# FNet mixing and a gated feed-forward on one core: where four units' halves of sums and two pairs' feed-forward operands stand

## The chip, the cores and the metric

The kernel runs on one core of a Trainium2 chip. Five engines work side by side, each through its own queue and in the order of its program: TensorE (PE) multiplies matrices, VectorE (DVE), ScalarE (ACT) and GpSimd (POOL) work on elements, SyncE (SP) starts the transfers. They wait for each other by semaphores; an instruction that waits holds up all that stands behind it in its queue. The metric is the device time of one execution in microseconds (us), lower is better.

## The reference

With S = 2048 rows, D = 448 columns and 1792 hidden columns:

```python
a = jnp.einsum("bsd,ed->bse", x, dft_hid_re)      # x is layernorm(A_x)
b = jnp.einsum("bsd,ed->bse", x, dft_hid_im)
y = jnp.einsum("ts,bse->bte", dft_seq_re, a) - jnp.einsum("ts,bse->bte", dft_seq_im, b)
...
h = A_x + y
g = jnp.einsum("bsd,df->bsf", x, w_gate)           # here x is layernorm(h)
u = jnp.einsum("bsd,df->bsf", x, w_up)
h2 = h + jnp.einsum("bsf,fd->bsd", gelu(g) * u, w_down)
```

The inputs are 32-bit floats, drawn at random; the four DFT matrices (cosines and sines) are inputs too.

## The kernel before

**Numbers.** Each 32-bit operand is split into two 16-bit halves: a high half, which ACT rounds (`hi_part`, L108), and a low half, the rest, which DVE subtracts (`lo_part`, L112 without and L114 with a scale). A product takes three matmuls: high by high, high by low, low by high.

**Stages.** First comes the sequence DFT: W (the cosine and sine matrices, `dft_seq`) times the normed rows xs. It runs in 64 steps, `for n in range(N_STEPS)`. Each step multiplies one *unit* of W, a 128 x 1024 piece that SP loads (`seq_load`, tile `wr`) and ACT and DVE split (tile `ws`). Then, pair by pair of row blocks (a pair p has the halves g = 0 and 1), comes the hidden DFT (`hid_mm(p, g)`, PE, L730, 21 matmuls). It follows in the same 64 steps as soon as a pair is through. Then the gate and up products and the down products run in two more loops, from about 346 us on.

**Units.** Up to step 27 a step is 24 plain matmuls (L644, tile `acc`). From `FAST` = 28 on a step is 42 matmuls of half the width (L521, tile `acc_f`) in Strassen's form: a unit has raw halves (`fast_raw`, tile `ws28_0` for unit 28, from `wr`) and four sums of its blocks (`fast_sums`, DVE, L471 to L473), whose halves `fast_split` makes (two ACT instructions and one of DVE, tile `ws28_1`). The other factor is xs, raw, and its sums T: for row pair j POOL adds (`t_sums(j)`, L575 to L581, tiles `tx`), ACT and DVE split (`t_hi(j)`, `t_lo(j)`, tile `t`). Step 28 reads T of j = 0 and 1, step 29 of 2 (first half) and 3 (second half), and so on. Units 28, 29 and 30 are made in steps 24, 26 and 27 (`fast_at`); from unit 31 on, unit n + 2 is made in step n. Of a unit's tile `wr` there are five buffers, which the sums share; of `ws` there are six.

**The hidden product's seed.** `hid_mm(p, g)` adds to a bank `y` that ACT fills before (`hid_seed(p, g)`, L711, scaled h). There is one such bank. So `hid_seed(p, 1)` waits until ACT has drained `hid_mm(p, 0)` (`hid_out`, L719 to L721), and `hid_mm(p, 1)` waits for the seed. For pair 1, `hid_mm(1, 0)` stands behind the first half of step 24, `hid_mm(1, 1)` behind the first half of step 25.

**Feed-forward operands.** For each of the first four pairs the normed h is made into operands of the gate and up products inside these steps: `ffn_norm_act` (ACT, L243), `ffn_sums` (six of DVE, L254 to L263, tile `tt`), `ffn_split` (four of ACT, six of DVE, tile `xs_`), `ffn_transpose` (four transposes of SP, L305). The steps stand in a table, `n0, n1, n2` for the normed h, the sums and the split; the transposes follow in steps n2 + 1 and n2 + 2.

**Order.** It is written by hand. In each step `n` all engines get, in this order: loads and halves of plain units; for `n in fast_at` the unit's sums and halves; what `early[n]` lists; the first half of the matmuls; `after[n, 0]`; the second half; `after[n, 1]`. Other work in these lists that the prediction speaks of: the gate weights (`Weights.sums`, `gu_s`, L328 to L331; `split`, `gu_w`), the drain of a finished plain pair (`z_out`, tile `zs`), SP's transposes of it (`z_turn`, L669), and the drain of a finished fast pair at the end of each fourth fast step (`fast_out`, tile `e`, L550 and L553). `t_hi(5)` stands in `after[24, 1]`, `t_hi(3)` in `after[27, 1]`, `t_lo(3)` in `after[28, 0]`.

Of the kernel before, what the change touches and what calls it, by code (L numbers as in the profile page):

```python
# [32 lines left out]
def kernel(  # L33
# [73 lines left out]
    def hi_part(dst, src, scale=1.0):  # L107
        A.activation(dst, src, AF.Copy, scale=scale)  # L108

    def lo_part(dst, src, hi, scale=1.0):  # L110
        if isinstance(scale, float) and scale == 1.0:
            V.tensor_sub(dst, src, hi)  # L112
        else:
            V.scalar_tensor_tensor(dst, src, scale, hi, op0=ALU.mult, op1=ALU.subtract)  # L114
# [304 lines left out]
    def step_of(n):  # L419

        k, qq = divmod(n - NT, 4)
        return 2 + k // 2, k % 2, qq

    def seq_load(n):
        wr[n] = dft.tile([P, 8 * P], F32, tag="wr", bufs=5, name=f"wr{n}")
        if n < NT:
            nc.sync.dma_start(wr[n].rearrange("p (b t) -> p b t", b=4), w_seq[8 * (n % 2) + n // 2])
            return
        p, part, qq = step_of(n)
        for i in range(2):  # L430
            dst = wr[n][:, i * 4 * P : (i + 1) * 4 * P].rearrange("p (g t) -> p g t", g=2)
            nc.sync.dma_start(dst, w_seq[8 * p + 2 * qq + i][:, 2 * part : 2 * part + 2, :])
# [19 lines left out]
    FAST = N_STEPS - 36  # L452
# [6 lines left out]
    def fast_views(n):  # L459
        raw = wr[n].rearrange("p (i b t) -> p i b t", i=2, b=4)  # L460
        s = fast_s[n].rearrange("p (s i t) -> p s i t", s=4, i=2)
        src = raw[:, :, 0:3].rearrange("p i b t -> p i (b t)")
        dst = fast_w[n][0][:, :, : 6 * P].rearrange("p l (i b) -> p l i b", i=2)
        return raw, s, src, dst
# [17 lines left out]
    def fast_raw(n):  # L482

        raw, s, src, dst = fast_views(n)
        hi_part(dst[:, 0], src, D_SC)
        lo_part(dst[:, 1], src, dst[:, 0], D_SC)

    def fast_split(n):

        w = fast_w[n][1]  # L490
        for part in slice(0, 4 * P), slice(4 * P, 8 * P):
            hi_part(w[:, 0, part], fast_s[n][:, part], D_SC)
        lo_part(w[:, 1], fast_s[n], w[:, 0], D_SC)
# [208 lines left out]
    def h_tile(q, j):  # L702
        hp[q, j] = pair_tile(f"hx{q}_{j}", 2 * (q - 2) + j if q > 1 else j)
        nc.sync.dma_start(hp[q, j], xr[q // 2, 2 * (q % 2) + j])
# [3 lines left out]
    def hid_seed(p, g):  # L708

        y = ys[p, g] = ps_tr.tile([P, 512], F32, tag="tr", name=f"y_{p}_{g}")  # L710
        A.activation(y[:, :D], hp[p // 2, p % 2][:, g, :], AF.Copy, scale=sign_of(p, g) * D_SC)  # L711
# [31 lines left out]
    def h_store(q, j):  # L743
        nc.sync.dma_start(h_dram[2 * q + j], hp[q, j])
# [10 lines left out]
    early, after = {}, {}  # L755

    def at(where, n, *what):
        where.setdefault(n, []).extend(what)
# [25 lines left out]
    for p, (n, half) in enumerate(turns):  # L784
        b, j = divmod(p, 2)
        m = (19, 24, 29, 36, 44, 52, 60)[p]
        last = ((20, 0), (25, 0), (31, 0), (38, 0), (48, 0), (56, 0), (61, 1))[p]
        m1 = last[0] + 1
        at(early, m - 4, lambda b=b, j=j: h_tile(b, j))
        at(early, m - 2, lambda p=p: hid_seed(p, 0))  # L790
        for g in range(2):

            place = last if g else (m, 0)
            at(after, place, lambda p=p, g=g: hid_mm(p, g), lambda p=p, g=g: hid_out(p, g))
            if g == 0:
                at(after, (m, 0), lambda p=p: hid_seed(p, 1))
        at(after, (n, half), lambda p=p: z_turn(p))
        at(early, m1 + p // 3 if p < 5 else N_STEPS - 7 + p, lambda b=b, j=j: ffn_rstd(b, j))
        at(after, (m1, 0), lambda b=b, j=j: h_store(b, j))
        if b < 2:  # L800

            n0, n1, n2 = ((21, 22, 23), (27, 28, 32), (36, 37, 38), (44, 45, 46))[p]
            at(early, n0, lambda b=b, j=j: ffn_bias(b, j), lambda b=b, j=j: ffn_norm_act(b, j, hp[b, j]))
            at(early, n1, lambda b=b, j=j: ffn_sums(b, j))
            at(early, n2, lambda b=b, j=j: ffn_split(b, j))
            for k in range(4):
                at(after, (n2 + 1 + k // 2, k % 2), lambda b=b, j=j, k=k: ffn_transpose(b, j, (k,)))
# [47 lines left out]
    for n in range(N_STEPS):  # L855
        if n == 0:
            for key in first:
                seq_acc(*key, last=key == first[-1])
        elif n >= FAST and n % 4 == 0:
            fast_begin(n)  # L860
        elif n >= NT and n % 4 == 0:
            for g in range(2):
                seq_acc(*step_of(n)[:2], g)
        if n + 3 < NT:
            x_load(n + 3)
        for unit in range(n + 5 + (n > FAST - 6), min(n + 6 + (n > FAST - 7), FAST + 2)):
            seq_load(unit)

        if 0 < n < FAST - 3:
            seq_hi(n + 3)  # L870
        if 0 < n < NT - 2:
            x_rstd(n + 2)
            x_hi(n + 2)
            x_norm(n + 2)
        if 0 < n < NT - 3:
            x_stats(n + 3)
        if n == 0:
            seq_lo(2)
        if n + 3 < FAST:
            seq_lo(n + 3)  # L880
        if n in fast_at:
            unit = fast_at.index(n) + FAST
            fast_sums(unit)
            while last_lo:
                last_lo.pop()()

            if n < FAST or n % 4 < 3:
                fast_raw(unit)
                fast_split(unit)
                if unit + 2 < N_STEPS:  # L890
                    seq_load(unit + 2)
        if n == 0:
            x_stats(3)
            x_lo(2)
        if 0 < n < NT - 2:
            x_lo(n + 2)
        for what in early.get(n, ()):
            what()
        if n >= FAST:

            last = n % 4 == 3
            one = [(i, k) for k in range(7) for i in range(2)] if last else [(i, k) for i in range(2) for k in range(7)]
            if n % 4 == 0 and n > FAST:

                one = [(i, k) for i in range(2) for k in range(5)] + [(i, k) for i in range(2) for k in (5, 6)]
            for m, (i, k) in enumerate(one):
                fast_mm(n, i, k)
                if last and i == 1 and k in (0, 2, 4, 6):  # L910
                    fast_out(n, k)
                    if n < N_STEPS - 1:
                        unit = n + 2
                        if k == 2:
                            fast_raw(unit)
                        elif k == 4:
                            fast_split(unit)
                            if unit + 2 < N_STEPS:
                                seq_load(unit + 2)
                if m in (6, 13):  # L920
                    for what in after.get((n, m // 7), ()):
                        what()
            continue

        if n < NT:
            one = [(key, n - n % 2 + key[0], 2 * (2 * key[1] + key[2]) + n % 2, n) for key in first]
            if n == 0:

                order = [(0, m) for m in (0, 2, 1)] + [(1, m) for m in range(3)]
                one = [(*a, (m,)) for jj, m in order for a in one[4 * jj : 4 * jj + 4]]  # L930
            elif n < 6:
                one = [(*a, (m,)) for m in (0, 2, 1) for a in one]
            else:
                one = [(*a, range(3)) for a in one]
        else:
            p, part, qq = step_of(n)
            one = [
                ((p, part, g), n, 4 * i + 2 * g + c, 4 * qq + 2 * i + c, range(3))
                for i in range(2)
                for g in range(2)  # L940
                for c in range(2)
            ]
            if qq == 3:

                one.sort(key=lambda a: a[0])
        for half in range(2):
            for key, unit, block, c, terms in one[half * len(one) // 2 : (half + 1) * len(one) // 2]:
                seq_mm(key, ws[unit], block, c, terms)
                if c == NT - 1 and 2 in terms and (n < NT or block in (5, 7)):
                    z_out(*key)  # L950
            for what in after.get((n, half), ()):
                what()
# [376 lines left out]
    for t in range(NF):  # L1329
        w = gu.get(t + 2) if t + 2 in JIT_F else None  # L1330
        n = PREP_AT.get(t)
# [88 lines left out]
    for t in range(NF, N_GU):  # L1420
# [37 lines left out]
        if ends:  # L1458
            p = now[-1] // NC
# [21 lines left out]
        for p, t0 in ended.items():  # L1481
            each = 3 if p < 3 else 2
            n = each * (t - t0)
# [106 lines left out]
```

## Time and profile before

| | us |
|---|---|
| time, median of 3 runs (709.05 to 711.11) | 709.29 |
| the profiled execution's own time | 708.99 |
| its span, first to last instruction | 707.2 |
| PE busy | 692.3 |
| DVE, ACT, POOL busy | 586.1, 397.4, 171.8 |

A row in order of time gives the start (us from the span's start), the length of the group of like instructions, engine, line, operation, what is written and read, its shape and the count; in brackets stand the idle time of the engine ahead of it and what ended it. The row of a group reaches to the end of its last instruction, and the next one of PE begins some 0.2 us before that, so stretches of PE are taken from start to start. Steps can be found by counting matmuls: 24 of L644 for a step up to 27, 42 of L521 from step 28, 21 of L730 for a hidden product.

### The profile page before, as it was taken

The page shows a single profiled execution, that of the slowest core. Times are in us where ns is not written, and L with a number is a line of the kernel's source. Part 1 is how long each engine was busy: PE and PEld are TensorE (multiplying, and loading weights), DVE is VectorE, ACT ScalarE, POOL GpSimd, SP SyncE. Part 2 cuts the span into 40 slices and gives each one's busy share as a digit, 9 for nine tenths or more (in the row PEclk, how much of TensorE's full clock was granted, in tenths as well). Part 3 has the DMA queues.
Part 4 walks back from the last instruction along what each step waited for, and adds up shares of the span by engine and source line. Part 5 has one row for each costly group of instructions (what it writes and reads, how often), then busy time and mean ns, then how long its engine had stood idle before and what let it go on. Part 6 is the DMA issues. An engine that isn't in the chain of part 4 may idle for free.

```text
span 707.2 us, 14130 instructions
## 1 busy us (share of the span) xinstructions
PE 692.3 (98%) x5380; PEld 521.2 (74%) x5380; DVE 586.1 (83%) x1156; ACT 397.4 (56%) x789; POOL 171.8 (24%) x183
## 2 busy tenths in 40 slices
PE   9999999599999999999999999999999999999998
PEld 6555555248888889888744444469999999999997
DVE  7998996969799899998576798877677876899886
ACT  5776655455566475654646666655546454555531
POOL 0005745732010100000213333511120111232224
PEclk9999999989999999999999999999999999999999
DMA  8788689883785829484775879797788985887612
GB/s 273 250 231 285 136 286 252 223 193 104 182 201 140 212 78 223 161 187 155 222 254 183 280 255 253 204 323 232 233 250 297 262 280 182 302 295 262 237 54 79
DMA packets 113444, 153.99 MB, mean 218 GB/s; under 512 B 61664, under 2 KB 78176, under 8 KB 113376
## 3 DMA queue, kind: packets, MB, share of 16 engines
q1 hardware_dynamic: 113376, 153.09, 72.5%
q8 instruction: 42, 0.69, 0.4%
q14 instruction: 26, 0.21, 0.1%
HBM read 104.82 MB, written 34.34 MB: 197 GB/s over the span
## 4 chain that ended last, share of the span: by engine, by line
PE 89%; DVE 6%; issue 2%; ACT 2%; DMA 1%; POOL 0%; SPq 0%; DVEq 0%; ACTq 0%; POOLq 0%
PE acc L644 17%; PE acc_d L1252 15%; PE acc_f L521 15%; PE pY L1048 15%; PE pX L1048 9%; PE pZ L1048 9%; PE y L730 8%; DVE ws L114 2%; DVE sums L471 1%; ACT ws L108 1%; PE pw L102 1%; DVE e L550 1%; DVE sums L472 1%; DMA wr<-in_w_seq_dram 1%; DVE xs L112 0%
## 5 line engine op out<-in xcount | busy, mean ns | idle before, releaser
L1048 PEld LDWEIGHTS <-gw 128*128 128x128 f16 x1287 | 125.8, 98 | 33.6
L521 PEld LDWEIGHTS <-ws 128*128 128x128 f16 x1512 | 144.7, 98 | 3.8 <-DVE ws L114 1.8
L644 PE MATMUL acc<-xs,ws 128*128 128x448 f16 x672 | 127.9, 352 | 0.0
L1142 POOL TENSOR_TENSOR hs<-hs,c 128x256 f32<-128x256 f32 (+1 forms) x42 | 61.3, 1460 | 244.7 <-ACT c L1140 192.5
L644 PEld LDWEIGHTS <-ws 128*128 128x128 f16 x672 | 65.7, 98 | 61.2
L1252 PE MATMUL acc_d<-wd,dn_w 128*128 128x224 f16 x1008 | 110.6, 259 | 0.0
L521 PE MATMUL acc_f<-t,ws 128*128 128x224 f16 x864 | 103.8, 259 | 0.4 <-DVE ws L114 0.4
L1252 PEld LDWEIGHTS <-dn_w 128*128 128x128 f16 x1008 | 96.9, 98 | 1.9
L114 DVE SCALAR_TENSOR_TENSOR ws<-wr,ws 128x768 f16<-128x768 f32 (+2 forms) x66 | 73.4, 1114 | 15.3 <-ACT ws L108 14.9
L521 PE MATMUL acc_f<-xs,ws 128*128 128x224 f16 x648 | 82.8, 259 | 0.7 <-DVE ws L114 0.7
L1048 PE MATMUL pY<-hops,gw 128*128 128x256 f16 (+1 forms) x561 | 81.9, 289 | 0.0
L730 PE MATMUL y<-wh,z 128*128 128x448 f16 x336 | 67.5, 357 | 9.2 <-ACT y L711 9.2
L1048 PEld LDWEIGHTS <-gu_w 128*128 128x128 f16 x351 | 34.2, 98 | 40.9
L108 ACT ACTIVATE ws<-wr 128x768 f16<-128x768 f32 (+2 forms) x66 | 59.4, 902 | 8.2 <-DMA wr<-in_w_seq_dram 6.9
L108 ACT ACTIVATE ws<-sums 128x512 f16<-128x512 f32 x72 | 43.4, 623 | 33.8 <-DVE sums L471 28.2
L730 PEld LDWEIGHTS <-z 128*128 128x128 f16 x336 | 33.2, 99 | 39.3 <-issue 11.0
L1048 PE MATMUL pX<-hops,gw 128*128 128x256 f16 (+1 forms) x363 | 56.3, 289 | 0.0
L1048 PE MATMUL pZ<-hops,gw 128*128 128x256 f16 (+1 forms) x363 | 56.3, 289 | 0.0
L1093 ACT ACTIVATE pY<-pX 128x256 f32<-128x256 f32 (+1 forms) x42 | 18.4, 439 | 65.4 <-PE pX L1048 65.0
L1058 DVE SCALAR_TENSOR_TENSOR c<-pZ,u 128x256 f32<-128x256 f32 (+1 forms) x42 | 21.4, 510 | 36.1 <-PE pZ L1048 19.4
L1104 ACT ACTIVATE u<-pY 128x256 f32<-128x256 f32 (+1 forms) x42 | 19.1, 454 | 53.5 <-PE pY L1048 53.4
L114 DVE SCALAR_TENSOR_TENSOR ws<-sums,ws 128x1024 f16<-128x1024 f32 x36 | 45.2, 1255 | 1.2 <-ACT ws L108 0.8
(148 smaller groups left out, 1039.9 us busy)
## 6 DMA issues: line engine op xcount, KB each, us to landing
gw<-w_dram SPq DMA_DIRECT2D x33, 896.0 KB, 6.4
wr<-in_w_seq_dram SPq DMA_DIRECT2D x100, 256.0 KB, 4.1
hid_dram<-hs SPq DMA_DIRECT2D x27, 512.0 KB, 6.0
hid<-hid_dram SPq DMA_DIRECT2D x54, 256.0 KB, 5.3
w_dram<-gu_w SPq DMA_DIRECT2D x14, 896.0 KB, 5.0
gu_raw<-in_w_gu_dram SPq DMA_DIRECT2D x28, 384.0 KB, 5.5
wr<-in_w_seq_dram SPq DMA_DIRECT2D x14, 512.0 KB, 5.0
x<-in_x_dram SPq DMA_DIRECT2D x16, 224.0 KB, 3.6
```

The source lines that it names most:

```text
L102: PE.transpose(pw[:, k % 8, :], ident, ident)
L108: A.activation(dst, src, AF.Copy, scale=scale)
L114: V.scalar_tensor_tensor(dst, src, scale, hi, op0=ALU.mult, op1=ALU.subtract)
L521: PE.matmul(fast_sum(n, k), fast_a(n, i, lw, a), fast_b(j, lx, b), start=j == 0 and m == 0 and k in (0, 1, 3, 5), stop=j == NT // 2 - 1 an ...
L644: PE.matmul(acc[key][:, :D], w[:, lw, block * P : (block + 1) * P], xs[c][:, lx, :], start=c == 0 and m == 0, stop=c == NT - 1 and m == 2,)
L730: PE.matmul(y[:, :D], z[p][:, lz, k, g * P : (g + 1) * P], wh[:, lw, k, :], start=p == NP - 1 and k == 0 and m == 0, stop=k == 6 and m == ...
L1048: PE.matmul(ps, w[:, wl, wa + ws, :], ops[:, m + ms, :], start=first and n == 0, stop=last and n == len(terms) - 1, skip_group_check=True,)
L1058: V.scalar_tensor_tensor(dst, ps, SC, other, op0=ALU.mult, op1=ALU.add)
L1093: A.activation(self.Y, self.X, AF.Copy)
L1104: A.activation(self.u2, self.Y, AF.Copy, scale=SC)
L1142: G.tensor_mul(c22, c22, self.cols(self.c12))
L1252: PE.matmul(ps, w[:, la, a, :], wd[n][:, lb, b, :], start=n == 0 and m == 0 and opens, stop=n == NC - 1 and m == 2, skip_group_check=True,)
```

## The change

```diff
-            n0, n1, n2 = ((21, 22, 23), (27, 28, 32), (36, 37, 38), (44, 45, 46))[p]
+            n0, n1, n2 = ((21, 25, 25), (27, 28, 32), (36, 37, 38), (44, 45, 48))[p]
...
-            if n < FAST or n % 4 < 3:
+            if n < FAST:
+                fast_raw(unit)
+                at(after, (n, 1), lambda unit=unit: fast_split(unit), lambda unit=unit: seq_load(unit + 2))
+            elif n % 4 < 3:
                 fast_raw(unit)
                 fast_split(unit)
                 if unit + 2 < N_STEPS:
```

In the steps below `FAST` (24, 26 and 27, so for units 28, 29 and 30) the halves of the sums and the load of the unit after next move from the step's start to the end of its second half, behind what `after[n, 1]` already lists. Pair 0's sums move from step 22 to 25 and its split from 23 to 25; the fourth pair's split (p = 3) moves from step 46 to 48. The transposes on SP follow their split. Nothing is added or taken away.

On ACT, this is the queue around step 24 before: the last of pair 0's activations (`xs_0_0<-tt_0_0`), the drain of `acc2`, units 27 and 28, the gate weights `gu_w5`, then the drain of `hid_mm(1, 0)` (`hx0_1`, `mv_h0_1`, `y_1_0`) and the seed (`y_1_1`).

```order
L108 ACTIVATE xs_0_0_1459<-tt_0_0_1404 128x192
L108 ACTIVATE zs2_1201<-acc2_10_1251 128x448
L108 ACTIVATE zs2_1201<-acc2_11_1252 128x448
L108 ACTIVATE ws27_1503<-wr27_1386 128x1024
L108 ACTIVATE ws28_0_1507<-wr28_1389 128x768
L108 ACTIVATE ws28_1_1508<-sums28_1506 128x512 x2
L108 ACTIVATE gu_w5_1454<-gu_s5_1399 128x512 x2
L719 ACTIVATE hx0_1_1268,mv_h0_1_1570<-y_1_0_1411 128x448
L720 ACTIVATE mv_h0_1_1570<-mv_h0_1_1570 128x1
L721 ACTIVATE y_1_0_1411,mv_h0_1_1570<-y_1_0_1411,mv_h0_1_1570 128x448
L711 ACTIVATE y_1_1_1574<-hx0_1_1268 128x448
```

The same place on ACT after the change, on to the first of pair 0's activations:

```order
L108 ACTIVATE ws27_1485<-wr27_1386 128x1024
L108 ACTIVATE ws28_0_1489<-wr28_1389 128x768
L108 ACTIVATE gu_w5_1447<-gu_s5_1399 128x512 x2
L719 ACTIVATE hx0_1_1268,mv_h0_1_1545<-y_1_0_1404 128x448
L720 ACTIVATE mv_h0_1_1545<-mv_h0_1_1545 128x1
L721 ACTIVATE y_1_0_1404,mv_h0_1_1545<-y_1_0_1404,mv_h0_1_1545 128x448
L711 ACTIVATE y_1_1_1549<-hx0_1_1268 128x448
L108 ACTIVATE t45_1438<-tx5_0_1500 128x448
L108 ACTIVATE t45_1438<-tx5_1_1501 128x448
L108 ACTIVATE ws28_1_1490<-sums28_1488 128x512 x2
L108 ACTIVATE xs_0_0_1578<-xn_h0_0_1355 128x256
```

Unit 28's halves (`ws28_1`) and pair 0's activations moved from ahead of the seed to behind it and behind `t_hi(5)` (`t45<-tx5`).

On ACT again, three steps on, at the end of step 27 before: unit 30's two tiles, pair 1's normed h (`xn_h0_1`), the seed of pair 2 (`y_2_0`), the drain of `acc3`, and `t_hi(3)` (`t2_3<-tx3`).

```order
L108 ACTIVATE ws30_0_1713<-wr30_1517 128x768
L108 ACTIVATE ws30_1_1714<-sums30_1712 128x512 x2
L243 ACTIVATE xn_h0_1_1727<-hx0_1_1268,mv_h0_1_1570,r_h0_1_1678 128x448 x2
L711 ACTIVATE y_2_0_1730<-hx1_0_1591 128x448
L108 ACTIVATE zs3_1753<-acc3_00_1501 128x448
L108 ACTIVATE zs3_1753<-acc3_01_1502 128x448
L108 ACTIVATE t2_3_1659<-tx3_0_1732 128x448
L108 ACTIVATE t2_3_1659<-tx3_1_1733 128x448
```

And on ACT there after the change:

```order
L108 ACTIVATE ws30_0_1711<-wr30_1568 128x768
L243 ACTIVATE xn_h0_1_1719<-hx0_1_1268,mv_h0_1_1545,r_h0_1_1668 128x448 x2
L711 ACTIVATE y_2_0_1722<-hx1_0_1589 128x448
L108 ACTIVATE zs3_1745<-acc3_00_1483 128x448
L108 ACTIVATE zs3_1745<-acc3_01_1484 128x448
L108 ACTIVATE t2_3_1655<-tx3_0_1724 128x448
L108 ACTIVATE t2_3_1655<-tx3_1_1725 128x448
L108 ACTIVATE ws30_1_1712<-sums30_1710 128x512 x2
```

Unit 30's halves moved from ahead of the normed h to behind `t_hi(3)`.

On DVE at the same place after the change, from unit 30's low half of sums to `t_lo(3)` in the last row; `gu_s0` are the gate sums of step 28 and `tt_0_1` pair 1's sums.

```order
L114 SCALAR_TENSOR_TENSOR ws30_1_1712<-sums30_1710,ws30_1_1712 128x1024
L328 TENSOR_TENSOR gu_s0_1776<-gu_raw0_1521 128x384
L329 TENSOR_TENSOR gu_s0_1776<-gu_s0_1776,gu_raw0_1521 128x384
L330 TENSOR_TENSOR gu_s0_1776<-gu_raw0_1521 128x256
L331 TENSOR_TENSOR gu_s0_1776<-gu_raw0_1521,gu_s0_1776 128x256
L254 TENSOR_TENSOR tt_0_1_1781<-xn_h0_1_1719 128x256
L256 TENSOR_TENSOR tt_0_1_1781<-xn_h0_1_1719,tt_0_1_1781 128x192
L257 TENSOR_SCALAR tt_0_1_1781<-tt_0_1_1781 128x64
L259 TENSOR_TENSOR tt_0_1_1781<-xn_h0_1_1719 128x192
L260 TENSOR_SCALAR tt_0_1_1781<-xn_h0_1_1719 128x64
L263 TENSOR_TENSOR tt_0_1_1781<-xn_h0_1_1719,tt_0_1_1781 128x192
L112 TENSOR_TENSOR t2_3_1655<-tx3_0_1724,t2_3_1655 128x448
```

Before, the first of these rows stood ahead of the two drains `zs3` as well, directly behind unit 30's raw low half; now it stands behind them and waits for the activations that follow `t_hi(3)` on ACT. The rest kept its order.

## The prediction

> **What bounds the kernel now.** I read the page first, then who waited for whom, then the PE rows of the one place that stands out.
>
> ```profile
> span 707.2 us, 14130 instructions
> ...
> PE 692.3 (98%) x5380; PEld 521.2 (74%) x5380; DVE 586.1 (83%) x1156; ACT 397.4 (56%) x789; POOL 171.8 (24%) x183
> ```
>
> PE is busy for 692.3 of 707.2 us, so without fewer matmuls only PE's waits can be won. The list of waits names them, longest in total first:
>
> ```profile
> PE y L730 <- ACT y L711: 9.2, 1, 9.2
> ...
> PE acc_f L521 <- DVE ws L114: 1.1, 2, 0.7
> ```
>
> The largest is one single wait: `hid_mm(1, 1)`, the second hidden product of pair 1, stands for `hid_seed(1, 1)`, which ACT writes (L711). PE's rows in order of time show the place and the stages after it:
>
> ```profile
> 98.41 4.70 PE L644 MATMUL acc<-xs,ws 128*128 128x448 f16 x24
> 102.95 4.13 PE L730 MATMUL y<-wh,z 128*128 128x448 f16 x21
> ...
> 125.08 4.14 PE L730 MATMUL y<-wh,z 128*128 128x448 f16 x21
> 129.06 4.70 PE L644 MATMUL acc<-xs,ws 128*128 128x448 f16 x24
> 142.94 5.48 PE L730 MATMUL y<-wh,z 128*128 128x448 f16 x21 [9.18 <-ACT y L711]
> 148.26 11.51 PE L644 MATMUL acc<-xs,ws 128*128 128x448 f16 x60
> 159.61 0.74 PE L521 MATMUL acc_f<-xs,ws 128*128 128x224 f16 x6
> ...
> 169.62 0.74 PE L521 MATMUL acc_f<-xs,ws 128*128 128x224 f16 x6
> ```
>
> Start to start, 24 matmuls take 4.54 us (98.41 to 102.95) and a hidden product 3.98 (125.08 to 129.06). Without the wait the 60 matmuls of steps 25 to 27 would start at 129.06 + 4.54 + 3.98 = 137.58; they start at 148.26. The wait costs **10.68 us**: the idle time, and 1.34 because the product behind it took 5.32 instead of 3.98.
>
> Why is the seed late? ACT's rows, then DVE's:
>
> ```profile
> 123.77 0.92 ACT L108 ACTIVATE gu_w<-gu_raw 128x512 f16<-128x512 f32 x2
> ...
> 128.19 0.96 ACT L108 ACTIVATE zs<-acc 128x448 f16<-128x448 f32 x2
> 129.03 1.78 ACT L108 ACTIVATE ws<-wr 128x1024 f16<-128x1024 f32 x2
> 137.53 0.63 ACT L108 ACTIVATE ws<-sums 128x512 f16<-128x512 f32 x1 [6.72 <-DVE sums L471]
> ...
> 139.67 1.13 ACT L108 ACTIVATE gu_w<-gu_s 128x512 f16<-128x512 f32 x2
> 140.71 0.52 ACT L719 ACTIVATE hx<-y 128x448 f32<-128x448 f32 x1
> ...
> 142.34 0.55 ACT L711 ACTIVATE y<-hx 128x448 f32<-128x448 f32 x1
> ```
>
> ```profile
> 123.75 1.25 DVE L254 TENSOR_TENSOR tt<-xn_h 128x256 f32<-128x256 f32 x1
> ...
> 127.34 1.68 DVE L114 SCALAR_TENSOR_TENSOR ws<-wr,ws 128x1024 f16<-128x1024 f32 x1
> ...
> 145.67 0.42 DVE L473 TENSOR_TENSOR sums<-wr,sums 128x256 f32<-128x256 f32 x1
> ```
>
> ACT's queue holds unit 28's halves of sums ahead of the seed and stands 6.72 us for DVE's sums (L471). DVE is late because pair 0's operands (L254 to L263, then a group at L112) lie ahead of those sums.
>
> **Part one: the wait goes.** In the new order neither pair 0's four activations nor unit 28's halves stand ahead of the seed. ACT is through with the raw gate weights at 124.69 (123.77 + 0.92); then follow zs 0.96, the two ws 1.78 and gu_w 1.13, to 128.6. The product whose result is drained ends at 129.22 (125.08 + 4.14); from L719 to the seed's start took 1.63 (140.71 to 142.34), the seed 0.55: ready at **131.4**. PE wants it at 129.06 + 4.54 = 133.60. With 2.2 us to spare, all 10.68 go.
>
> **What is late next.** PE then starts step 28 at 137.58 + 11.35 = 148.93 (148.26 to 159.61 is 11.35), and the second half of step 29, behind `hid_mm(2, 0)`, 10.01 later (159.61 to 169.62) at 158.94. The eighth matmul of that half reads the low halves of T for row pair 3 (`t_lo(3)`); seven take 0.67, so they are due at **159.6**. What stands ahead of them:
>
> ```profile
> 154.03 0.16 DVE L203 RECIPROCAL r_h<-sd_h 128x2 f32<-128x2 f32 x1
> ...
> 163.98 0.58 DVE L254 TENSOR_TENSOR tt<-xn_h 128x256 f32<-128x256 f32 x1
> ...
> 165.62 1.15 DVE L112 TENSOR_TENSOR t<-tx,t 128x448 f16<-128x448 f32 x2
> ```
>
> ```profile
> 156.77 3.72 POOL L575 TENSOR_TENSOR tx<-xs 128x448 f32<-128x448 f16 x2
> ```
>
> ```profile
> 164.72 0.58 ACT L108 ACTIVATE t<-tx 128x448 f16<-128x448 f32 x1 [2.07 <-POOL tx L581]
> ```
>
> Before: the reciprocal at 154.03, Pool's sums from 156.77 until they release ACT at 164.72, ACT's high half done at 165.30, `t_lo(3)` at 166.77, 3.5 us ahead of its use (169.62 + 0.67). Two things change.
>
> First, the reciprocal moves earlier by less than PE does. DVE's work from 123.75 to the end of unit 29's sums at 146.09 (145.67 + 0.42), 22.3 us, is the same set in another order. Pair 0's six sums, 3.59 us beside a busy Pool (123.75 to 127.34), should cost the 1.64 of pair 1's (163.98 to 165.62) where they now stand, but what lies beside Pool instead gets slower. So unit 29's sums end between 144.2 and 146.1; I take 145.1, the middle. With one raw half of 0.95 ahead of it (row below) the reciprocal is at 146.0: 8.0 us earlier, where PE is 10.7 earlier.
>
> Second, unit 30's halves now stand on ACT behind `t_hi(3)`, which waits for Pool; and DVE's low half of unit 30 stands ahead of the gate sums, pair 1's sums and `t_lo(3)`. DVE reaches it at about 154 and idles until ACT is through, with that other work behind it. From the reciprocal: 11.27 to the end of `t_hi(3)` as before (154.03 to 165.30), then the high halves, the low half, the gate sums, pair 1's sums and `t_lo(3)`.
>
> ```profile
> 106.32 0.56 DVE L328 TENSOR_TENSOR gu_s<-gu_raw 128x384 f32<-128x384 f32 x1
> ...
> 107.73 0.42 DVE L331 TENSOR_TENSOR gu_s<-gu_raw,gu_s 128x256 f32<-128x256 f32 x1
> ...
> 168.21 0.95 DVE L114 SCALAR_TENSOR_TENSOR ws<-wr,ws 128x768 f16<-128x768 f32 x1
> 169.08 1.22 DVE L114 SCALAR_TENSOR_TENSOR ws<-sums,ws 128x1024 f16<-128x1024 f32 x1
> ```
>
> ```profile
> 151.71 1.14 ACT L108 ACTIVATE ws<-sums 128x512 f16<-128x512 f32 x2
> ```
>
> 1.14 + 1.22 + 1.83 (gate sums, 106.32 to 108.15) + 1.64 + 1.15 = 6.98. So 146.0 + 11.27 + 6.98 = 164.25; as Pool is less disturbed while DVE idles I take 164.0. Due 159.6: **a new wait of 4.4 us** in step 29. Bounds: 2.7 (unit 29's sums at 144.2, Pool's 7.9 us a tenth shorter) and 6.5 (sums at 146.1, Pool a tenth longer and no relief).
>
> **Then nothing more.** Behind `t_lo(3)` DVE needs 3.5 us for unit 31 (166.77 to 170.30); PE first has 14 matmuls and step 30, 5.4 us. In step 31 the drain is where DVE stood for PE:
>
> ```profile
> 182.71 1.05 DVE L550 SCALAR_TENSOR_TENSOR e<-acc_f,e 128x224 f32<-128x224 f32 x2 [3.43 <-PE acc_f L521]
> ```
>
> Those 3.43 us are DVE's reserve. `t_lo(3)` was 3.5 ahead of PE and is now on time at best, so the reserve is just used up, and from here both run as before, 6.3 us earlier. What it falls short comes off the gain.
>
> **The fourth pair.** Its halves move from step 46 to 48, and its transposes on SP behind z's and between W's loads. One small wait rests on it:
>
> ```profile
> 262.02 0.42 DVE L112 TENSOR_TENSOR xs<-xn_h,xs 128x256 f16<-128x256 f32 x1
> 264.10 0.69 DVE L471 TENSOR_TENSOR sums<-wr 128x512 f32<-128x512 f32 x1
> ```
>
> ```profile
> 274.00 1.16 PE L521 MATMUL acc_f<-t,ws 128*128 128x224 f16 x9
> ```
>
> The low halves (262.02 to 264.10) push unit 50 by 2.1 us, and nine matmuls take 1.16 at step 50 where 1.03 is usual: 0.1 to win. The 1.1 us of waits for ws come at step 48, ahead of the moved work, and stay. Bounds: 0.5 either way, as a W load may land earlier or later.
>
> Pair 0's transposes and the loads of units 31 and 32 I cost at nothing. Unit 31's load now stands on SP behind z's transposes, which wait for the product that ends at 137.6, and behind two of pair 0's:
>
> ```profile
> 148.45 5.25 SPq L669 DMA_TRANSPOSE z<-zs  x4
> ```
>
> With 5.25 for z's and half as much for the two, it is issued near 147, and DVE asks for it at 164.
>
> **Sum.** The profiled execution took 708.99 us (span 707.2), 0.3 below the median 709.29. 708.99 − 10.68 + 4.4 − 0.1 = **702.6**; by the bounds of the new wait 700.9 to 704.7.
>
> **Rivals.** (1) *The new wait also lowers the clock.* The granted clock around the old wait (stretch, its length, PE busy, clock, DMA share, GB/s):
>
> ```profile
> 133.70:138.70 5.00, 0.06 (x1) 1.00 1.17 214
> 138.70:139.20 0.50, 0.00 (x0) 0.68 0.70 251
> ...
> 142.90:145.90 3.00, 2.96 (x9) 0.53 0.58 223
> ```
>
> The clock fell to half 5.1 us after the last matmul (about 138.9 against 133.8) and stayed there until 145.8. A wait of 4.4 ends just before that. If it is 5, or the fall is not counted from the last matmul, the next matmuls run at half clock and lose up to the 1.34 above: 708.99 − 10.68 + 4.9 + 1.3 − 0.1 = 704.4. [...]
>
> (2) *No new wait.* If DVE and Pool get to row pair 3 four us sooner, the whole 10.7 remain: 698.2. For it: DVE idles beside Pool, whose two additions took 3.72 beside a busy DVE. Against it: two other groups stand ahead of `t_lo(3)` on DVE.
>
> (3) *Slower.* If pair 0's transposes hold up SP, unit 31's load lands late and step 31 waits. PE wants unit 31 at 164.0 + 5.4 = 169.4, DVE needs 3.5 for it: the load decides from 165.9 on. To end over 0.3% slower it must eat the gain of 6.4 and 2.1 more, so land near 174.4: 711.1 or more. Nothing in SP's rows holds it that long.
>
> (4) *The seed stays late.* If a load, zs or the gate weights hold ACT, part of the old wait remains. It costs from 2.2 us on, the wait for `t_lo(3)` shrinks by as much, and only from 8.6 us of it on the result is no change: 706.9 to 709. ACT waited for none of them in these rows.
>
> **How the numbers follow.** Forecast 0.55; lower clock 0.22; no new wait 0.13; seed late 0.05; slower 0.05. The range goes from the case without a wait to just above the clock's: 698.1 to 705.4. Less than 0.3%, 2.1 us, can't be told from no change. Faster 0.90 (the first three), same 0.05, slower 0.05.
>
> **What would show it.** The 9.2 us of L730 on L711 are gone; in their place PE (L521) stands 3 to 6 us for DVE (L112, tile t) near 160; DVE idles some 4 us before 158, ended by ACT's ws (L108); from step 31 on the same rows come 6 us earlier, the 1.1 us at step 48 among them. I am wrong if PE stands at L730 again, if there is no wait near 160, or if waits for ws (L114) come in steps 33 to 44, where DVE has no gap.

## The result, and the profile after

| | us |
|---|---|
| before, median of 4 runs beside the changed kernel (709.05 to 711.11) | 709.79 |
| changed kernel, median of 4 runs (703.78 to 704.78) | 704.05 |
| ratio, 95% interval | 0.9919 [0.9901, 0.9937] |
| forecast, range | 702.6, 698.1 to 705.4 |
| profiled execution of the changed kernel, its span | 704.78, 703.0 |

The kernel is faster, by 0.8%, and the time lies in the range, 1.5 us above the forecast. The profiled execution is the slowest of the four; its mean granted clock is 0.995, that of the other three 0.997 to 0.998. Its page:

```profile
span 703.0 us, 14133 instructions
...
PE 693.5 (99%) x5380; PEld 522.5 (74%) x5380; DVE 585.8 (83%) x1156; ACT 397.2 (57%) x789; POOL 172.5 (25%) x183
```

PE's work grew by 1.2 us (692.3 to 693.5) with the same 5380 matmuls: something made some of them slower. Who PE waited for, in the changed kernel:

```profile
PE acc_f L521 <- DVE t L112: 4.4, 1, 4.4
...
PE acc_f L521 <- DVE ws L114: 0.2, 1, 0.2
```

The wait at L730 is gone, a new one of 4.4 us for tile t is there, and the 1.1 us for ws are down to 0.2. ACT's rows at the place of the old wait, in order of time:

```profile
129.93 0.54 ACT L719 ACTIVATE hx<-y 128x448 f32<-128x448 f32 x1 [1.06 <-PE y L730]
...
131.59 0.55 ACT L711 ACTIVATE y<-hx 128x448 f32<-128x448 f32 x1
```

ACT is now early and stands for PE, not the other way round. The seed is ready at 132.14 (131.59 + 0.55). PE's rows:

```profile
129.67 4.70 PE L644 MATMUL acc<-xs,ws 128*128 128x448 f16 x24
134.21 4.14 PE L730 MATMUL y<-wh,z 128*128 128x448 f16 x21
138.18 11.51 PE L644 MATMUL acc<-xs,ws 128*128 128x448 f16 x60
...
159.54 0.74 PE L521 MATMUL acc_f<-xs,ws 128*128 128x224 f16 x6
160.12 0.26 PE L521 MATMUL acc_f<-t,ws 128*128 128x224 f16 x1
164.79 1.65 PE L521 MATMUL acc_f<-t,ws 128*128 128x224 f16 x8 [4.42 <-DVE t L112]
...
170.10 0.45 PE L521 MATMUL acc_f<-xs,ws 128*128 128x224 f16 x3
```

PE takes the seed at 134.21 without a break. The new wait ends at 164.79, in front of the eighth matmul of the second half of step 29. The 29 matmuls from there to 170.10 take 5.31 us, where seven take 0.67 elsewhere, so 29 would take 2.78: **2.5 us more are lost behind the wait.** The windows of the changed kernel say why (stretch, its length, busy time of PE, weight loads, DVE, ACT, POOL, then the granted clock):

```profile
160.50:163.00 2.50, 0.00 (x0) 0.00 (x0) 2.43 (x8) 0.00 (x0) 0.00 (x0) 1.00 0.00 0
163.00:163.50 0.50, 0.00 (x0) 0.00 (x0) 0.50 (x4) 0.00 (x0) 0.00 (x0) 0.70 0.00 0
163.50:170.00 6.50, 5.21 (x29) 4.10 (x29) 6.40 (x12) 4.24 (x11) 0.00 (x0) 0.50 0.25 78
```

The clock falls to half near 163.2, during the wait, and stays there until 170. DVE's rows from the reciprocal to `t_lo(3)`:

```profile
147.53 0.16 DVE L203 RECIPROCAL r_h<-sd_h 128x2 f32<-128x2 f32 x1
...
153.90 1.14 DVE L114 SCALAR_TENSOR_TENSOR zs<-acc,zs 128x448 f16<-128x448 f32 x2
159.24 1.23 DVE L114 SCALAR_TENSOR_TENSOR ws<-sums,ws 128x1024 f16<-128x1024 f32 x1 [4.20 <-ACT ws L108]
...
163.59 1.16 DVE L112 TENSOR_TENSOR t<-tx,t 128x448 f16<-128x448 f32 x2
```

DVE stands 4.20 us for ACT, in front of unit 30's low half, and the gate sums, pair 1's sums and `t_lo(3)` follow behind it. That is the shape the prediction gave. The drain of step 31 and the wait at step 48:

```profile
179.74 1.05 DVE L550 SCALAR_TENSOR_TENSOR e<-acc_f,e 128x224 f32<-128x224 f32 x2 [2.71 <-PE acc_f L521]
```

```profile
258.12 0.84 PE L521 MATMUL acc_f<-t,ws 128*128 128x224 f16 x7 [0.19 <-DVE ws L114]
...
259.38 4.14 PE L730 MATMUL y<-wh,z 128*128 128x448 f16 x21
```

**Where the time went**, profiled execution against profiled execution. PE comes to step 25 0.61 later (129.67 against 129.06; the nine profiles of this study have this row between 128.88 and 129.82, the kernel before within that, so nothing of the change can be read from it). Old wait with the slowed product −10.68, new wait +4.42, half clock +2.53, waits at step 48 −0.90 (1.09 to 0.19), small rest behind them −0.2, of which 0.1 at step 50: together −4.2, from 708.99 to 704.78. The medians differ by 1.5 more, 5.7: the profiled execution of before lies below its four runs in the table, that of the changed kernel is the slowest of its four.

### The profile page after: what moved, and what is told of

It reads as the page before. It is cut to its first block, busy times and chain, and to the rows that moved or that the text cites. A ratio compares the mean times of both kernels' runs of the same rounds, so it can differ in the third digit from the quotient of the medians.

```text
span 703.0 us, 14133 instructions
## 1 busy us (share of the span) xinstructions
PE 693.5 (99%) x5380; PEld 522.5 (74%) x5380; DVE 585.8 (83%) x1156; ACT 397.2 (57%) x789; POOL 172.5 (25%) x183
## 4 chain that ended last, share of the span: by engine, by line
PE 72%; DVE 14%; DMA 5%; issue 3%; ACT 2%; SPq 2%; POOL 1%; DVEq 0%; ACTq 0%; POOLq 0%
PE acc_d L1255 15%; PE pY L1051 15%; PE acc_f L521 14%; PE pX L1051 10%; PE pZ L1051 10%; PE y L730 6%; DVE ws L114 4%; DMA x<-in_x_dram 3%; PE acc L644 3%; DMA wr<-in_w_seq_dram 2%; DVE xs L112 1%; DVE sums L471 1%; DVE st_x L122 1%; ACT ws L108 1%; SPq L669 1%
## 5 line engine op out<-in xcount | busy, mean ns | idle before, releaser
L521 PE MATMUL acc_f<-t,ws 128*128 128x224 f16 x864 | 105.7, 262 | 4.6 <-DVE t L112 4.4
L730 PE MATMUL y<-wh,z 128*128 128x448 f16 x336 | 66.2, 353 | 0.0
L108 ACT ACTIVATE ws<-wr 128x768 f16<-128x768 f32 (+2 forms) x66 | 59.4, 902 | 6.4 <-DMA wr<-in_w_seq_dram 4.1
L108 ACT ACTIVATE ws<-sums 128x512 f16<-128x512 f32 x72 | 43.1, 622 | 28.0 <-DVE sums L471 22.6
L730 PEld LDWEIGHTS <-z 128*128 128x128 f16 x336 | 32.8, 98 | 29.0
```

Source lines behind the costliest of these rows:

```text
L521: PE.matmul(fast_sum(n, k), fast_a(n, i, lw, a), fast_b(j, lx, b), start=j == 0 and m == 0 and k in (0, 1, 3, 5), stop=j == NT // 2 - 1 an ...
L730: PE.matmul(y[:, :D], z[p][:, lz, k, g * P : (g + 1) * P], wh[:, lw, k, :], start=p == NP - 1 and k == 0 and m == 0, stop=k == 6 and m == ...
```

## The experiments

Each was run beside runs of the kernel before on the same chip. Four went first (before: 708.84, median of 7), three later (before: 709.14, median of 13). The changed kernel had 709.79 beside it, 0.95 more than in the first group. So kernels of different groups are also compared by their gains on before: the median of before beside each kernel, less its own.

**1. Unit 30's halves back at the step's start.** Is the new wait made by where unit 30's halves stand? Against the changed kernel:

```diff
-            if n < FAST:
+            if n < FAST - 1:
                 fast_raw(unit)
                 at(after, (n, 1), lambda unit=unit: fast_split(unit), lambda unit=unit: seq_load(unit + 2))
-            elif n % 4 < 3:
+            elif n < FAST or n % 4 < 3:
```

> Theory A (order): the new wait of 4.4 us in step 29 is there because unit 30's halves stand on ACT behind t_hi(3) and DVE idles 4.2 us with the gate sums and pair 1's sums behind it. With unit 30's halves back at the start of step 27, DVE does that work while Pool adds; t_lo(3) then follows t_hi(3) (near 158.2) or DVE's own queue (near 161) and is due near 160.4: a wait of 0 to 1 us, no fall of the clock, 698 to 700 us. Theory B (Pool is too late): with PE 10 us earlier, Pool's sums for row pair 3 come too late in any order; the wait stays at 3 us or more and the time at 702 to 704.

Measured: 698.85 (698.73 to 699.71), ratio 0.9857 [0.9842, 0.9871]. PE's wait in this kernel, then its DVE rows:

```profile
PE acc_f L521 <- DVE t L112: 1.2, 1, 1.2
```

```profile
155.21 1.14 DVE L114 SCALAR_TENSOR_TENSOR zs<-acc,zs 128x448 f16<-128x448 f32 x2
156.27 0.68 DVE L328 TENSOR_TENSOR gu_s<-gu_raw 128x384 f32<-128x384 f32 x1
...
160.12 1.16 DVE L112 TENSOR_TENSOR t<-tx,t 128x448 f16<-128x448 f32 x2
...
173.74 1.05 DVE L550 SCALAR_TENSOR_TENSOR e<-acc_f,e 128x224 f32<-128x224 f32 x2 [0.18 <-PE acc_f L521]
```

DVE goes from the drain to the gate sums without a gap, `t_lo(3)` is done at 161.28 instead of 164.75, the wait is 1.2 us (0 to 1 was expected), and the granted clock is 1.0 throughout. Less wait (3.2) and no half clock (2.5) make 5.7 in the profiles; the medians differ by 5.2, the gains on before by 4.3 (10.0 against 5.7). The edit puts unit 32's load back as well, but DVE's idle time was ended by ACT's halves (`ACT ws L108`), so it is the order of unit 30's halves that is shown to make most of the wait. This kernel beats both.

**2. The halves alone** (the table of before) **and 3. the first pair alone** (the branch of before). Which of the two removes the old wait? Against the kernel before, 2 has the diff's second part only, 3 has this:

```diff
-            n0, n1, n2 = ((21, 22, 23), (27, 28, 32), (36, 37, 38), (44, 45, 46))[p]
+            n0, n1, n2 = ((21, 25, 25), (27, 28, 32), (36, 37, 38), (44, 45, 46))[p]
```

> Only the halves of units 28 to 30 move; pair 0's and the fourth pair's operands stand as before. If the halves alone held the seed, it is ready near 134.1, as ACT's pair-0 activations and their wait for DVE (1.8 us) are still ahead: a wait of 0.5 us at the hidden product of step 25, then again some 4 us at step 29: 703.5 to 705. If pair 0's operands are needed too for the seed to be in time, PE waits at L730 for 3 us or more and the time is above 705.

> Only pair 0's operands move to step 25; unit 28's halves still stand on ACT ahead of the seed and wait for DVE's sums. Those sums start 3.6 to 5.7 us earlier on DVE, so the seed is ready near 137.7 and PE waits some 4 us at the hidden product of step 25 instead of 9.2. Unit 30's halves are not moved: by theory A no wait at step 29. 702 to 704 us. By theory B a wait of some 2 us at step 29 comes on top.

Measured: the halves alone 705.21 (704.61 to 705.49), ratio 0.9943 [0.9928, 0.9958]; the first pair alone 704.46 (703.16 to 705.54), 0.9933 [0.9916, 0.9949]. PE's waits with the halves alone, then with the first pair alone:

```profile
PE acc_f L521 <- DVE t L112: 3.9, 1, 3.9
...
PE acc_f L521 <- DVE ws L114: 1.1, 2, 0.7
...
PE y L730 <- ACT y L711: 0.2, 1, 0.2
```

```profile
PE y L730 <- ACT y L711: 4.9, 1, 4.9
...
PE acc_f L521 <- DVE ws L114: 0.4, 1, 0.4
```

The halves alone take the old wait from 9.2 to 0.2 and bring the new one; the first pair alone takes it to 4.9 and brings none. The first pair's part is needed only for the last 0.2, as the halves are what ACT stood for. By the medians the halves alone gain 3.6 us, the first pair alone 4.4 and both together 5.7 (intervals that overlap): what the halves gain is partly paid back in step 29. Both times lie above the expected ranges, by 0.2 and 0.5 us; with the first pair alone the wait was 4.9 and not some 4. The wait of 4.9 in the first-pair kernel costs more than its length, too:

```profile
138.75 6.76 PE L730 MATMUL y<-wh,z 128*128 128x448 f16 x21 [4.90 <-ACT y L711]
145.35 11.51 PE L644 MATMUL acc<-xs,ws 128*128 128x448 f16 x60
```

The product takes 6.60 start to start, not 3.98: 2.6 us of half clock.

**4. The wait filled with work.** Is the half clock a cost of its own? The changed kernel with 46 matmuls ahead of the waiting one; they add to a half of a bank that nothing reads, and are no part of what is computed.

```diff
             for m, (i, k) in enumerate(one):
+                if n == FAST + 1 and i == 1 and k == 2:
+                    for _ in range(46):
+                        PE.matmul(
+                            fast_acc[FAST][0][:, HD:D],
+                            fast_a(n, 1, 0, "A11"),
+                            fast_b(3, 0, "B11"),
...
                 fast_mm(n, i, k)
```

> The changed kernel with 46 more matmuls (the rows of unit 29 by high halves of xs, written to an unused half of a bank) in step 29 ahead of the matmul that waits, about 4.4 us at full rate: PE has work where it waited. If the wait alone costs, the time is that of the changed kernel, 704 us, or a little more. If the fall of the clock costs up to 2.5 us on top (29 matmuls in 5.3 us in the changed kernel's profile), the granted clock stays at 1.00 and the time falls by 1 to 2.5 us: 701.5 to 703.

Measured: 701.86 (701.47 to 703.77), ratio 0.9906 [0.9889, 0.9922] to the kernel before; the changed kernel had 0.9919 [0.9901, 0.9937]. The intervals overlap, so the time alone doesn't decide; the profile does. PE's rows and one of DVE in the filled kernel:

```profile
159.35 4.57 PE L914 MATMUL acc_f<-xs,ws 128*128 128x224 f16 x46
163.76 1.22 PE L521 MATMUL acc_f<-t,ws 128*128 128x224 f16 x9
164.81 0.45 PE L521 MATMUL acc_f<-xs,ws 128*128 128x224 f16 x3
```

```profile
176.46 1.05 DVE L550 SCALAR_TENSOR_TENSOR e<-acc_f,e 128x224 f32<-128x224 f32 x2 [0.17 <-PE acc_f L521]
```

The stretch is as long as the wait was, but the next nine matmuls take 1.05 us start to start, where nine of the changed kernel's take 1.65 (5.31 / 29 each), and the granted clock of this profile is 1.0. The half clock is a cost of its own. DVE's idle time ahead of the drain of step 31 shows it a second time: 0.17 here, 2.71 in the changed kernel. The 2.5 us that PE lost there gave DVE 2.5 us more of reserve.

How much the half clock costs is less certain: 2.5 us by the matmuls behind the wait, 2.2 by the medians, 1.2 by the gains on before (7.0 against 5.7). The profile of the changed kernel shows the costlier case. In its three other executions a mean clock of 0.997 to 0.998 over some 702 us makes 3 to 4 us at half clock, by estimate, about half of the profile's 6.8. The kernel with the halves alone has such a profile (0.998): there the 29 matmuls took 4.43 (164.26 to 168.69) and lost 1.65. So some 1.7 us is the estimate for the median of the changed kernel.

**5. The fourth pair alone, 6. the fourth pair put back.** Does its move change the wait at step 48? Number 5 is the kernel before with (44, 45, 48) alone; number 6 is experiment 1 with (44, 45, 46):

```diff
-((21, 22, 23), (27, 28, 32), (36, 37, 38), (44, 45, 46))[p]
+((21, 22, 23), (27, 28, 32), (36, 37, 38), (44, 45, 48))[p]
```

```diff
-((21, 25, 25), (27, 28, 32), (36, 37, 38), (44, 45, 48))[p]
+((21, 25, 25), (27, 28, 32), (36, 37, 38), (44, 45, 46))[p]
```

> The kernel before with the fourth pair's halves alone at step 48 instead of 46. Two theories of the wait for ws at step 48, which was 1.1 us before, 1.1 with the halves of W alone moved (fourth pair at 46), 0.4 with the first pair alone moved (fourth pair at 46) and 0.2 in the changed kernel. Theory A (prediction): the fourth pair is worth 0.1 us, its wait does not depend on it: the wait at step 48 stays at 0.7 + 0.4 us and the time is the kernel's before within 0.5 us, some 708.5 to 709.5. Theory B: the fourth pair's transposes on SP stood ahead of W's loads there; moved, the loads of units 48 and 49 are issued behind one another and the wait at step 48 shrinks to 0.2 us: 0.9 us faster, some 707.5 to 708.2. PE's wait at L730 stays 9.2 us under both.

> The kernel with unit 30's halves at the step's start, and the fourth pair's halves back at step 46, so that only the first pair and units 27 to 29 are changed from the kernel before. Theory A (the fourth pair is worth 0.1 us): 698.8 to 699.3, the wait for ws at step 48 stays at 0.3 to 0.4 us. Theory B (the fourth pair takes the wait away): the wait at step 48 is back at 1.1 us and the time 0.8 us longer, some 699.5 to 700.

Measured: alone 709.58 (708.47 to 710.38), ratio 1.0005 [0.9995, 1.0014], which is no change; put back 699.74 (699.11 to 700.16), 0.9863 [0.9847, 0.988], which can't be told from experiment 1. (The text on number 6 says units 27 to 29; the halves moved in it are those of 28 and 29.) Two rows and a wait of the first kernel:

```profile
142.75 6.65 PE L730 MATMUL y<-wh,z 128*128 128x448 f16 x21 [9.18 <-ACT y L711]
149.24 11.51 PE L644 MATMUL acc<-xs,ws 128*128 128x448 f16 x60
```

```profile
PE acc_f L521 <- DVE ws L114: 0.4, 1, 0.4
```

The wait at step 48 fell by 0.7, yet the profiled time is that of before (708.97). In this profile the product behind the old wait took 6.49, against 5.32 in the profile of before, with the same wait of 9.18: the half clock's cost varied by 1.2 us and covered the rest. Neither theory of the text fits whole: the wait shrank, the time did not.

With the fourth pair at step 46 the wait at step 48 was 1.1, 1.1, 0.4 and 0.8 in four profiles, with it at 48 between 0 and 0.4 in five. But the moved halves stand behind unit 48's halves in DVE's queue (before: 262.02 behind 260.89), so they can't hold those up. What the wait goes with is a load of W some 19 us earlier, for which DVE stands in step 44; before, then with the fourth pair alone:

```profile
242.26 0.69 DVE L471 TENSOR_TENSOR sums<-wr 128x512 f32<-128x512 f32 x1 [3.22 <-DMA wr<-in_w_seq_dram]
```

```profile
242.38 0.69 DVE L471 TENSOR_TENSOR sums<-wr 128x512 f32<-128x512 f32 x1 [2.36 <-DMA wr<-in_w_seq_dram]
```

Reckoned from PE's row of 18 matmuls in step 43 (237.02 and 238.00), these sums begin 5.24 and 4.38 later. In the nine profiles it was 5.24 and 5.27 where the wait at step 48 was 1.1, 4.97 where it was 0.8, 4.39 (first pair alone, halves at 46) and 4.38 (halves at 48) where it was 0.4, and 4.11 to 4.28 where it was 0 to 0.3. So this wait follows the load, with the halves in either place; why the load comes sooner in some kernels stays open. What the move itself does shows at step 50, where nine matmuls took 1.15 or 1.16 in all four profiles with the halves at 46 and 1.02 or 1.03 in all five with them at 48; in the changed kernel:

```profile
269.97 1.03 PE L521 MATMUL acc_f<-t,ws 128*128 128x224 f16 x9
```

That is 0.1 us, too little for the times of experiments 5 and 6 to show.

**7. Pair 1's sums behind `t_lo(3)`.** Against experiment 1:

```diff
-((21, 25, 25), (27, 28, 32), (36, 37, 38), (44, 45, 48))[p]
+((21, 25, 25), (27, 29, 32), (36, 37, 38), (44, 45, 48))[p]
```

> The kernel with unit 30's halves at the step's start, and pair 1's sums at step 29 instead of 28, so that they stand behind t_lo(3) on DVE. Theory: what is left of the wait in step 29 (1.2 us) is DVE's queue ahead of t_lo(3), which holds pair 1's sums of 1.6 us; then it shrinks to some 0.3 us, bounded by Pool and ACT (high half of t(3) done 159.1, low half 1.15 behind it, due at 160.0), and the time falls by 0.9 us from 698.9 to some 697.5 to 698.2. Rival: DVE has no room behind t_lo(3), and the 1.6 us come back as a wait for unit 31 or 32's tiles in step 31 or 32: no change or up to 1 us slower, 698.7 to 700.

Measured: 697.59 (697.22 to 697.86), ratio 0.9836 [0.9821, 0.985]. DVE's rows of this kernel, then PE's:

```profile
158.12 0.41 DVE L331 TENSOR_TENSOR gu_s<-gu_raw,gu_s 128x256 f32<-128x256 f32 x1
158.45 1.15 DVE L112 TENSOR_TENSOR t<-tx,t 128x448 f16<-128x448 f32 x2
...
173.10 1.04 DVE L550 SCALAR_TENSOR_TENSOR e<-acc_f,e 128x224 f32<-128x224 f32 x2
```

```profile
159.04 0.74 PE L521 MATMUL acc_f<-xs,ws 128*128 128x224 f16 x6
159.62 1.03 PE L521 MATMUL acc_f<-t,ws 128*128 128x224 f16 x9
```

The nine matmuls run through: the rest of the wait is gone. By the medians it gains 1.3 us on experiment 1, by the gains on before 1.6, where 0.9 was expected; the two intervals overlap, but the wait is gone from the profile, and none came back behind it, though the drain of step 31 has no idle time left ahead of it. This is the fastest kernel of the study, 1.6% under the kernel before.

## Why the prediction was right, point by point

- **The old wait goes, −10.68: right.** The seed was forecast for 131.4 and came at 132.14, with PE 0.6 later too; 2.1 us to spare where 2.2 were forecast. That the moved halves are the larger cause is shown by experiments 2 and 3.
- **A new wait of 4.4 us for `t_lo(3)`: right in place, cause and size, 4.42.** The cause is shown by experiment 1, its last part by experiment 7. Two sub-terms were off and cancelled. The reciprocal came at 147.53, 0.9 later than 146.0 beside PE's own 0.6, as unit 29's sums ended not in the middle of their range but at its upper bound (146.75, less 0.6, against 146.1). From it to the end of `t_lo(3)` it took 17.22, where the sum had 18.25 and the prediction took 18.0: Pool and ACT needed 10.64 to the end of `t_hi(3)` (158.17) instead of 11.27 (Pool's rows of L579 and L580 took 0.66 each beside the idle DVE, 0.85 and 0.72 before beside a busy one), the rest 6.58 instead of 6.98. That the size came out to 0.02 is luck.
- **Then nothing more, DVE's reserve just used up: right.** With the clock held (experiment 4) DVE had 0.17 us left at the drain of step 31, in experiment 1 0.18. That the changed kernel shows 2.71 is the slowed PE.
- **The clock: the step that failed.** The prediction said "A wait of 4.4 ends just before that" and gave the half clock a chance of 0.22. The clock fell 2.8 us after the last matmul (160.4 to 163.2), not 5.1. One interval of one profile had been taken for a constant, and so the forecast had nothing for the clock. The rival named the lower clock; its 1.3 was the old wait's loss, and it measured 2.5 in the profiled execution, with 1.7 the estimate for the median. The filled kernel, with the wait's length and no half clock, took 701.86, the forecast being 702.6; the changed kernel took 704.05, the rival having 704.4.
- **The fourth pair, −0.1: right, "and stay" wrong.** The nine matmuls at step 50 lost their 0.1. The waits at step 48 did not stay: they fell by 0.9 in the changed kernel, more than the bound of 0.5, as a load of W came sooner (experiments 5 and 6). That made up a third of the clock's 2.5 in the profile, which helped the time to land 1.5 from the forecast and not further off. That is luck as far as is known, since what moved the load stays open.
- **Pair 0's transposes and unit 31's load at nothing: right.** The load was issued at 149.46, forecast near 147, and DVE began unit 31's sums directly behind `t_lo(3)`:

```profile
149.46 1.66 SPq L432 DMA_DIRECT2D wr<-in_w_seq_dram  x2
```

## What to carry to other kernels

A wait that is removed is worth its length, and the slowed work behind it, only up to the next wait on the path: work the due time of the next operand and what stands ahead of it in each in-order queue, and don't move work that is ready behind one that waits. PE waits of 3.9 to 9.2 us cost a half clock of their own in these profiles, of 1.3 to 2.6 us, which varied between executions of like waits; waits of 1.2 us cost none. For a new wait of 4 us it belongs in the main sum, not in a rival. Where a moved piece makes the new wait, put that piece alone back: here unit 30's halves put back, and then pair 1's sums moved behind `t_lo(3)`, doubled the gain, from 0.8% to 1.6%.

## What the runs showed of the hardware

In these profiles the clock did not fall at a fixed time after the last matmul. It fell 5.1 us after it before (133.8 to 138.9), 2.8 in the changed kernel (160.4 to 163.2), about 4.1 with the fourth pair alone (133.6 to some 137.6), and with the halves alone even after PE had begun again. The windows of that last kernel, as above:

```profile
162.00:164.00 2.00, 0.00 (x0) 0.00 (x0) 1.97 (x7) 0.00 (x0) 0.00 (x0) 1.00 0.00 0
164.00:164.50 0.50, 0.24 (x3) 0.24 (x3) 0.50 (x2) 0.00 (x0) 0.00 (x0) 1.00 0.00 0
164.50:165.00 0.50, 0.50 (x6) 0.42 (x4) 0.47 (x2) 0.10 (x1) 0.00 (x0) 0.56 0.00 0
165.00:167.50 2.50, 2.50 (x16) 1.94 (x15) 2.47 (x4) 2.27 (x5) 0.00 (x0) 0.50 0.00 0
167.50:168.00 0.50, 0.50 (x5) 0.42 (x3) 0.50 (x2) 0.44 (x3) 0.00 (x0) 0.53 0.27 70
```

PE runs from 164.26, the clock falls at some 164.6 and is back near 168.0, after 3.4 us. Before (138.9 to 145.7) and in the changed kernel (163.2 to 170.0) it stayed low for some 6.8 us. With the first pair alone it is an estimate: the mean clock of 0.995 is that of both these profiles, so some 6.8 us again, and the 2.6 us lost from 138.75 on make half clock until some 144.0; the fall then came about 3.4 us after the last matmul (133.85). With the fourth pair alone the low stretch was some 10.2, from 137.6 to 147.9:

```profile
137.50:138.00 0.50, 0.00 (x0) 0.00 (x0) 0.50 (x1) 0.48 (x1) 0.42 (x2) 0.64 0.98 380
147.50:148.00 0.50, 0.50 (x3) 0.24 (x2) 0.00 (x0) 0.00 (x0) 0.00 (x0) 0.62 0.07 22
```

That is why the same wait of 9.18 us cost 2.5 us of slowed matmuls there and 1.34 before: PE began again at 142.75 and 142.94, with half clock until 147.9 there and until some 145.7 before.

What sets the moment of the fall and the length of the low stretch, these runs do not show.
